# A fused attention and mixture-of-experts kernel: attention in two-bank PSUM tiles, three banks for the second layer, folds in quarters, and batch 1 turned by transfers

## The chip, the cores and the metric

The kernel runs on one core of a Trainium2 chip. The metric is device time in microseconds of one execution (us); lower is better. The profile is one execution recorded by the hardware profiler; its span is a little shorter than the device time of the same execution (543.2 against 544.93 us for the kernel before). In this text PE is TensorE (PEld its weight loads), DVE is VectorE, ACT is ScalarE, POOL is GpSimd and SP is SyncE. In code and profile extracts `...` marks what was left out.

## The reference, cut to what matters

Eight batches of pooled attention, then four experts with two layers each on the 4,608 resulting rows.

```python
# q, k, v: (8 batches, 8 heads, 576, 64)
k_p = k.reshape(B, H, 72, 8, D).mean(axis=3)          # keys and values pooled by 8
v_p = v.reshape(B, H, 72, 8, D).mean(axis=3)
scores = scale * np.matmul(q, k_p.transpose(0, 1, 3, 2))
attn = softmax(scores)                                # exp, divided by its sum
x = (attn @ v_p)  -> transposed to (4608, 512)
# w1: (4, 512, 1024), w2: (4, 1024, 512), p: (4608, 4), normalized
for e in range(4):
    out += p[:, e:e+1] * (np.maximum(x @ w1[e], 0) @ w2[e])
```

## The kernel before

Each batch is a chunk of 512 rows (the 64 rows left of each batch are gathered into a ninth chunk). The experts' matmuls run as a stream. The attention of the next batch is cut into "pieces" that are strewn between the matmuls of the current one, some per slot; there are 32 slots in a chunk (4 experts, 2 halves, 4 gaps).

The PSUM pools have three tiles of one bank each for attention, three for the first layer and two for the second layer:

```python
psum_a = ...tile_pool(name="psum_a", bufs=3, space=PSUM)   # attention
psum_h = ...tile_pool(name="psum_h", bufs=3, space=PSUM)   # first layer
psum_o = ...tile_pool(name="psum_o", bufs=2, space=PSUM)   # second layer
```

Pooling ("folding") keys and values is additions on VectorE. Keys and queries must then be turned; for batches 2 and later a transposing transfer of the DMA engines does it, for batches 0 and 1 TensorE does it and VectorE copies the result out of PSUM:

```python
def by_dma(b):
    return b >= 2

def fold_keys(b, hs):
    raw = raws[("kraw", b)]
    fold(raw, hs)                                  # two additions: 8 -> 4 -> 2
    for dup in range(2):
        nc.vector.tensor_add(out=kps[b % 2][0:SP, hs, dup, :], in0=raw[:, hs, 0, :], in1=raw[:, hs, 1, :])

def keys(b, hs):
    ...
    if by_dma(b):
        nc.sync.dma_start_transpose(out=state[("kpT", b)][:], in_=kps[b % 2][:]...)
        return
    kpt_ps = psum_a.tile([P, H, SP], BF16, tag="a", name="kpt_ps")
    for h in range(hs.start, hs.stop):
        nc.tensor.transpose(kpt_ps[:, h, :], kps[b % 2][0:SP, h], ident[:SP, :SP])
    nc.vector.tensor_copy(out=state[("kpT", b)][:, hs, 0:SP], in_=kpt_ps[:, hs])
# queries(b, pair) and turn(b, r) do the same for q_sb -> qT and for x_tok -> xT

def scores(b, pair):
    both = [psum_a.tile([P, 2, 2, P], F32, tag="a", name="sc_ps") for _ in range(2)]
    ...                                            # four matmuls into the two banks
    exps(b, pair, 0)                               # one exp of 512 for each bank

def divide(c_ps, x_tok, half):                     # one for each half of the heads
    nc.vector.reciprocal(out=inv[:], in_=c_ps[:, :, D])
    nc.vector.tensor_tensor(out=x_tok[:, half], in0=c_ps[:, :, 0:D], in1=inv..., op=ALU.mult)
```

The pieces of a batch:

```python
def opening():
    if by_dma(b): queries(b, 0)
    fold_keys(b, every)                            # all eight heads at once
    if by_dma(b): keys(b, every); load_next()
add(opening)
add(folded_values)                                 # fold_values(b, every), then load_v(b + 1)
if by_dma(b):
    for _ in range(3): add(lambda: None)           # time for the transfers
else:
    add(lambda: keys(b, every)); add(lambda: queried(0))
for pair in range(NPAIR): ...                      # scores, second exp
for r in range(NR): ...                            # contexts, divisions, turning
add(lambda: combine_x(b))                          # the sums of x that the first layer needs
```

The first layer takes seven products in place of eight (`up_seven`). Its result leaves PSUM through ACT copies and through VectorE operations that write `H_sb`; the next products wait for those to free their bank. The weight sums for the products are made on VectorE by `combine_w1(e)`, once per expert, during the first chunk.

The loads are issued on POOL, whose queue is worked in this order:

```python
load_k(0); load_q(0); load_v(0); load_w1(0); load_probs(); load_w1(1); load_w2(0)
load_w1(2); load_w2(1); load_w1(3)
attention_first(); norm_probs(); combine_x(0)
load_k(1); load_q(1); load_v(1); load_w2(2); load_w2(3); load_q_rem(0); load_q_rem(1)
```

The softmax here doesn't subtract the row's maximum and nothing guards it: scores larger than these inputs give would overflow.

## Time and profile before

| | before |
|---|---|
| device time, median of the first 3 runs | 547.04 us (545.41 to 547.12) |
| span of the profiled run | 543.2 us |
| PE busy | 511.9 us, 94% |
| VectorE busy | 322.4 us, 59% |
| PE waits that the waits view lists | kpT's fold 14.4 us, H_sb 4.1 us, others about 8 us |

Three lines of the profile page of the kernel before: busy time by engine, the clock granted to TensorE in 40 equal slices of the span (tenths of full speed), and the chain of work that ended last, as shares of the span.

```profile
PE 511.9 (94%) x3736; PEld 328.7 (61%) x3736; DVE 322.4 (59%) x599; ACT 233.5 (43%) x403; POOL 45.7 (8%) x64
...
PEclk9999899999999999999999999999999999999999
...
PE 84%; DVE 9%; DMA 5%; issue 1%; ACT 0%; POOL 0%; POOLq 0%; DVEq 0%
```

TensorE is the bound. A change can gain only where PE waits, so the next view is the one to read. It is the waits of PE in the kernel before: what waited, for what, then total us, times, longest us.

```profile
PE kpt_ps L182 <- DVE kp L169: 14.4, 3, 7.8
PE g_ps L432 <- DVE H_sb L470: 4.1, 6, 0.8
```

Of the 14.4 us, 10.7 are at the very start; the third one is 3.68 us at 50.6 us, where batch 1's attention starts. The six waits for H_sb come one for each of the batches 2 to 7 (at 106, 155, 219, 268, 331 and 380 us), where the folds of the next batch's keys and values stand between VectorE's H_sb operations.

The same place by stretches of 10 us (busy us and instructions of each engine, then granted clock, DMA share, GB/s), kernel before:

```profile
core 0: us, PE busy (x) PEld busy (x) DVE busy (x) ACT busy (x) POOL busy (x), PEclk, DMA share, GB/s
50.00:60.00 10.00, 5.97 (x32) 3.32 (x30) 6.26 (x10) 0.97 (x2) 0.54 (x1) 0.66 1.30 201
60.00:70.00 10.00, 9.50 (x74) 5.87 (x75) 6.18 (x12) 6.25 (x12) 2.71 (x4) 1.00 1.20 170
70.00:80.00 10.00, 8.76 (x84) 5.90 (x83) 9.08 (x22) 3.22 (x6) 0.00 (x0) 1.00 1.05 126
```

A share of 1.0 and more (with 201, 170 and 126 GB/s) says that the DMA engines are busy throughout until 80 us: the weights of the experts and batch 1's q, k, v are still coming.

### The profile page before, as it was taken

Reading aid. Unit: us, or ns where it says so; the run is one execution under the profiler, and the core shown is the slowest. Engines: PE = TensorE matmul, PEld = TensorE weight load, DVE = VectorE, ACT = ScalarE, POOL = GpSimd, SP = SyncE. Lnnn points to the kernel's source line nnn. Section 1 sums busy time; section 2 is a strip of 40 time slices with the busy share of each in tenths; the row PEclk is TensorE's granted clock in tenths of the full one; section 3 lists DMA queues with packets and bytes.
Section 4 is the critical chain, followed back from the end, with each engine's and each line's share of the span. In section 5 each row is a group of like instructions: output and inputs, shape, how many; then the busy total and the mean of one; then the engine's idle time right before and its main releaser. Section 6 shows DMA issues by size and latency. Waiting matters only on the chain.

```text
span 543.2 us, 9149 instructions
## 1 busy us (share of the span) xinstructions
PE 511.9 (94%) x3736; PEld 328.7 (61%) x3736; DVE 322.4 (59%) x599; ACT 233.5 (43%) x403; POOL 45.7 (8%) x64
## 2 busy tenths in 40 slices
PE   2696999999999999999999999999999999999996
PEld 1354556566656666566666665666566666666663
DVE  3725588837773767367836665568456644554453
ACT  1463343473346333643373345533653345334430
POOL 6632100200110000201100002000000000000000
PEclk9999899999999999999999999999999999999999
DMA  8999980681781014914831119331101010011003
GB/s 122 197 206 200 196 109 1 136 133 31 93 152 38 19 21 111 153 28 70 121 90 23 28 51 165 65 69 32 59 17 25 35 53 1 11 40 39 2 1 77
DMA packets 72954, 40.98 MB, mean 75 GB/s; under 512 B 42688, under 2 KB 68288, under 8 KB 72912
## 3 DMA queue, kind: packets, MB, share of 16 engines
q0 software_dynamic: 33744, 22.63, 29.2%
q1 hardware_dynamic: 39168, 17.77, 14.0%
q8 instruction: 29, 0.48, 0.4%
q14 instruction: 13, 0.11, 0.1%
HBM read 45.16 MB, written 9.44 MB: 101 GB/s over the span
## 4 chain that ended last, share of the span: by engine, by line
PE 84%; DVE 9%; DMA 5%; issue 1%; ACT 0%; POOL 0%; POOLq 0%; DVEq 0%
PE o_ps L501 41%; PE g_ps L432 36%; DMA vraw<-in_v_dram 4%; PE sc_ps L221 2%; DVE H_sb L470 2%; DVE acc L515 2%; PE h_ps L450 2%; PE c_ps L249 1%; DMA kraw<-in_k_dram 1%; DVE vraw L157 1%; DVE kraw L157 1%; DVE vraw L159 1%; PE xt_ps L261 1%; DVE kp L169 1%; DVE x_tok L236 0%
## 5 line engine op out<-in xcount | busy, mean ns | idle before, releaser
L501 PE MATMUL o_ps<-w_bf,H_sb 128*128 128x512 bf16 x1152 | 295.6, 380 | 0.0
L470 DVE CUSTOM_DVE_ANT_0 H_sb<-g_ps,r 128x512 bf16<-128x512 f32 x210 | 143.8, 687 | 162.6 <-ACT r L466 90.3
L432 PEld LDWEIGHTS <-w_bf 128*128 128x128 bf16 x1960 | 185.3, 98 | 75.7 <-issue 11.7
L466 ACT COPY r<-g_ps 128x512 f32<-128x512 f32 x210 | 123.1, 586 | 208.4 <-PE g_ps L432 206.7
L432 PE MATMUL g_ps<-xf,w_bf 128*128 128x256 bf16 x1120 | 157.6, 274 | 6.4 <-DVE H_sb L470 4.1
L501 PEld LDWEIGHTS <-H_sb 128*128 128x128 bf16 x1152 | 113.0, 98 | 76.6 <-issue 0.8
L432 PE MATMUL g_ps<-xT,w_bf 128*128 128x256 bf16 x744 | 101.8, 273 | 0.0
L515 DVE SCALAR_TENSOR_TENSOR acc<-o_ps,p_all,acc 128x512 f32<-128x512 f32 x108 | 80.5, 746 | 21.1 <-PE o_ps L501 21.1
L487 ACT ACTIVATE H_sb<-g_ps 128x512 bf16<-128x512 f32 x70 | 41.8, 598 | 48.2 <-PE g_ps L432 48.2
L228 ACT ACTIVATE expT<-sc_ps 72x512 bf16<-72x512 f32 x64 | 37.1, 592 | 12.5 <-PE sc_ps L221 12.3
L236 DVE TENSOR_TENSOR x_tok<-c_ps,inv 128x256 bf16<-128x256 f32 x72 | 30.6, 425 | 2.5
L92 POOL DMA_DIRECT2D q_sb<-in_q_dram x9 | 7.9, 876 | 237.1 <-DMA qT<-q_sb 230.2
L512 ACT ACTIVATE acc<-o_ps,p_all 128x512 f32<-128x512 f32 x36 | 24.9, 691 | 4.7 <-PE o_ps L501 4.7
L249 PEld LDWEIGHTS <-expT 72*128 72x128 bf16 x256 | 16.2, 102 | 15.3 <-issue 3.1
L235 DVE RECIPROCAL inv<-c_ps 128x4 f32<-128x4 f32 x72 | 12.7, 177 | 14.6 <-PE c_ps L249 11.9
L249 PE MATMUL c_ps<-vp,expT 72*128 72x65 bf16 x256 | 18.4, 200 | 2.8 <-DVE vp L188 2.5
L221 PE MATMUL sc_ps<-qT,kpT 64*72 64x256 bf16 x128 | 14.5, 298 | 1.4 <-DVE qT L210 0.9
L182 PE MATMUL kpt_ps<-ident,kp 72*128 72x72 bf16 x16 | 1.5, 251 | 14.4 <-DVE kp L169 14.4
L221 PEld LDWEIGHTS <-kpT 64*72 64x72 bf16 x128 | 5.4, 111 | 13.8 <-issue 12.9
L157 DVE TENSOR_TENSOR kraw<-kraw 72x2048 bf16<-72x2048 bf16 (+1 forms) x9 | 9.9, 1096 | 5.8 <-DMA kraw<-in_k_dram 5.8
L432 PE MATMUL g_ps<-x_rem,w_bf 128*128 128x256 bf16 x96 | 13.3, 273 | 0.0
L157 DVE TENSOR_TENSOR vraw<-vraw 72x2048 bf16<-72x2048 bf16 (+1 forms) x9 | 9.9, 1095 | 3.7 <-DMA vraw<-in_v_dram 3.7
(54 smaller groups left out, 140.9 us busy)
## 6 DMA issues: line engine op xcount, KB each, us to landing
out_dram<-acc SPq DMA_DIRECT2D x32, 256.0 KB, 2.5
w_bf<-in_moe_w_dram POOLq DMA_DIRECT2D x16, 256.0 KB, 11.3
w_bf<-in_moe_w_dram POOLq DMA_DIRECT2D x4, 1024.0 KB, 18.3
kraw<-in_k_dram POOLq DMA_DIRECT2D x7, 576.0 KB, 10.3
vraw<-in_v_dram POOLq DMA_DIRECT2D x7, 576.0 KB, 11.8
q_sb<-in_q_dram POOLq DMA_DIRECT2D x7, 512.0 KB, 6.9
out_dram<-acc SPq DMA_DIRECT2D x8, 128.0 KB, 2.3
kraw<-in_k_dram POOLq DMA_DIRECT2D x2, 288.0 KB, 5.8
```

What stands on the lines that cost most here:

```text
L157: nc.vector.tensor_add(out=raw[:, hs, 0:4, :], in0=raw[:, hs, 0:4, :], in1=raw[:, hs, 4:8, :])
L221: nc.tensor.matmul(both[r2][0:SP, hh], lhsT=kpT[lo:lo + D, h, 0:SP], rhs=qT[lo:lo + D, h])
L228: nc.scalar.activation(out=state[("expT", b)][:, 2 * pair:2 * pair + 2, :, r2, :], in_=state[("sc", b, pair)][r2][0:SP], func=ACT.Exp, sca ...
L236: nc.vector.tensor_tensor(out=x_tok[:, half], in0=c_ps[:, :, 0:D], in1=inv[:].unsqueeze(2).to_broadcast([P, NPAIR, D]), op=ALU.mult,)
L249: nc.tensor.matmul(c_ps[:, i, :], lhsT=expT[:, h, r // 2, r % 2, :], rhs=vp[:, h, :])
L432: nc.tensor.matmul(bank[:, t, :], lhsT=w1_bf[:, e, block, kc, lo:lo + P], rhs=x[:, kc, :], start=(first and t == 0 and kc == 0), stop=(t = ...
L466: nc.scalar.copy(out=r[:], in_=ps[:])
L470: nc.vector._custom_dve(TENSOR_ADD_SAT, out=out, in0=ps[:], in1=r[:], s0=BIG, s1=0.0)
L487: nc.scalar.activation(out=low[:, :, 0:TH], in_=g[:], func=ACT.Relu)
L501: nc.tensor.matmul(sums[r][:], lhsT=hidden[(c, e)][:, fc, r * P:(r + 1) * P], rhs=w2_bf[:, e, fc, :], start=(fc == 0), stop=(fc == FCH - 1),)
L512: nc.scalar.activation(out=accs[(c, r)][:], in_=o_ps[:], func=ACT.Copy, scale=prob)
L515: nc.vector.scalar_tensor_tensor(out=dst, in0=o_ps[:], scalar=prob, in1=dst, op0=ALU.mult, op1=ALU.add,)
```

## The change

The intent: use one instruction over two banks where there were two (one exp of 1024, one reciprocal and one multiply per row block); free one bank for a third tile of the second layer; spread the burst of folds over four pieces; and take batch 1's turning off TensorE and VectorE by letting the DMA engines do it. The core of the diff:

```diff
-psum_a bufs=3, psum_o bufs=2
+psum_a bufs=1, psum_o bufs=3              # one attention tile, of two banks
+    def two_banks():
+        return psum_a.tile([P, 2, NT], F32, tag="a", name="two")

     def by_dma(b):
-        return b >= 2
+        return b >= 1

     scores:
-        both = [psum_a.tile([P, 2, 2, P], F32, tag="a", name="sc_ps") for _ in range(2)]
+        two = two_banks()
         ... four matmuls ...
+        nc.scalar.activation(out=dst, in_=two[0:SP]..., func=ACT.Exp, scale=EXP_SCALE)

-    def divide(c_ps, x_tok, half):          # twice per row block
+    def divide(banks, x_tok):               # once per row block, both banks
+        nc.vector.reciprocal(out=inv[:], in_=c_ps[:, :, :, D])
+        nc.vector.tensor_tensor(out=x_tok[:], in0=c_ps[:, :, :, 0:D], in1=inv..., op=ALU.mult)

     attention(b):
-        add(opening)                        # query transfer, fold of all keys, key transfer
-        add(folded_values)
+        add(lambda: (turn_queries(), fold_keys(b, lo)))
+        add(keyed)                          # fold_keys(b, hi), key transfer, load_next
+        add(lambda: fold_values(b, lo))
+        add(folded_values)                  # fold_values(b, hi), load_v(b + 1)
     # [cut: half of the first batch's score and context tiles come from the other two pools;
     #  the remainder chunks likewise use the two-bank tile]
```

What stays TensorE's to turn (the first batch's keys and x) takes its tiles from the attention pool as before, so those now come from the single two-bank tile.

More of the change, by code (lines that the diff above doesn't have):

```diff
@@ L60 @@
     rpool = ctx.enter_context(tc.tile_pool(name="rpool", bufs=6))
-    psum_a = ctx.enter_context(tc.tile_pool(name="psum_a", bufs=3, space=bass.MemoryType.PSUM))
+    psum_a = ctx.enter_context(tc.tile_pool(name="psum_a", bufs=1, space=bass.MemoryType.PSUM))
     psum_h = ctx.enter_context(tc.tile_pool(name="psum_h", bufs=3, space=bass.MemoryType.PSUM))
-    psum_o = ctx.enter_context(tc.tile_pool(name="psum_o", bufs=2, space=bass.MemoryType.PSUM))
+    psum_o = ctx.enter_context(tc.tile_pool(name="psum_o", bufs=3, space=bass.MemoryType.PSUM))
     w1_bf = wpool.tile([P, E, 7, 2, FH], BF16, name="w1_bf")
@@ L154, with one_bank @@
     state = {}
+    def two_banks():
+        return psum_a.tile([P, 2, NT], F32, tag="a", name="two")
+    def one_bank(n):
+        pool, tag = ((psum_h, "h_ps"), (psum_o, "o_ps"))[n % 2]
+        return pool.tile([P, NT], F32, tag=tag, name="one")
     def fold(raw, hs):
@@ L215, in scores @@
             state[("expT", b)] = apool.tile([SP, H, 2, 2, P], BF16, name="expT", bufs=1)
-        both = [psum_a.tile([P, 2, 2, P], F32, tag="a", name="sc_ps") for _ in range(2)]
+        expT = state[("expT", b)]
+        apart = b == 0 and pair % 2
+        if apart:
+            both = [one_bank(n)[:] for n in range(2)]
+        else:
+            two = two_banks()
+            both = [two[:, n] for n in range(2)]
         for hh in range(2):
@@ L221, in scores, with divide_half @@
                 nc.tensor.matmul(
-                    both[r2][0:SP, hh], lhsT=kpT[lo:lo + D, h, 0:SP], rhs=qT[lo:lo + D, h]
-                )
-        state[("sc", b, pair)] = both
-        exps(b, pair, 0)
-    def exps(b, pair, r2):
+                    both[r2][0:SP].rearrange("j (h r p) -> j h r p", h=2, r=2)[:, hh],
+                    lhsT=kpT[lo:lo + D, h, 0:SP], rhs=qT[lo:lo + D, h],
+                )
+        dst = expT[:, 2 * pair:2 * pair + 2].rearrange("j h r s p -> j s (h r) p")
+        if apart:
+            for n in range(2):
+                nc.scalar.activation(
+                    out=dst[:, n], in_=both[n][0:SP].rearrange("j (a p) -> j a p", p=P),
+                    func=ACT.Exp, scale=EXP_SCALE,
+                )
+            return
         nc.scalar.activation(
-            out=state[("expT", b)][:, 2 * pair:2 * pair + 2, :, r2, :],
-            in_=state[("sc", b, pair)][r2][0:SP], func=ACT.Exp, scale=EXP_SCALE,
-        )
-    def divide(c_ps, x_tok, half):
-        inv = npool.tile([P, NPAIR], F32, name="inv")
+            out=dst, in_=two[0:SP].rearrange("j s (a p) -> j s a p", p=P),
+            func=ACT.Exp, scale=EXP_SCALE,
+        )
+    def divide(banks, x_tok):
+        c_ps = banks[:, :, 0:NPAIR * (D + 1)].rearrange("p a (h d) -> p a h d", h=NPAIR)
+        inv = npool.tile([P, 2, NPAIR], F32, name="inv")
+        nc.vector.reciprocal(out=inv[:], in_=c_ps[:, :, :, D])
+        nc.vector.tensor_tensor(
+            out=x_tok[:], in0=c_ps[:, :, :, 0:D],
+            in1=inv[:].unsqueeze(3).to_broadcast([P, 2, NPAIR, D]), op=ALU.mult,
+        )
+    def divide_half(bank, x_tok, half):
+        c_ps = bank[:, 0:NPAIR * (D + 1)].rearrange("p (h d) -> p h d", h=NPAIR)
+        inv = npool.tile([P, NPAIR], F32, name="invh")
         nc.vector.reciprocal(out=inv[:], in_=c_ps[:, :, D])
@@ L239, in divide, with context_half @@
         )
-    def context(b, r, half):
+    def context_half(b, r, half, bank):
         expT, vp = state[("expT", b)], vps[b % 3]
-        if ("x", b, r) not in state:
-            state[("x", b, r)] = npool.tile([P, 2, NPAIR, D], BF16, name="x_tok", bufs=5)
-        pool, tag = (psum_h, "h_ps") if b == 0 and half else (psum_a, "a")
-        c_ps = pool.tile([P, NPAIR, D + 1], F32, tag=tag, name="c_ps")
         for i in range(NPAIR):
@@ L249, in context, with context_first @@
             nc.tensor.matmul(
-                c_ps[:, i, :], lhsT=expT[:, h, r // 2, r % 2, :], rhs=vp[:, h, :]
-            )
-        divide(c_ps, state[("x", b, r)], half)
+                bank[:, i * (D + 1):(i + 1) * (D + 1)],
+                lhsT=expT[:, h, r // 2, r % 2, :], rhs=vp[:, h, :],
+            )
+    def context(b, r):
+        x_tok = npool.tile([P, 2, NPAIR, D], BF16, name="x_tok", bufs=5)
+        state[("x", b, r)] = x_tok
+        banks = two_banks()
+        for half in range(2):
+            context_half(b, r, half, banks[:, half])
+        divide(banks, x_tok)
+    def context_first(r, half):
+        if half == 0:
+            state[("x", 0, r)] = npool.tile([P, 2, NPAIR, D], BF16, name="x_tok", bufs=5)
+        bank = one_bank(r)
+        context_half(0, r, half, bank[:])
+        divide_half(bank[:], state[("x", 0, r)], half)
     def flip(x_tok, dst, on_dma, copy=nc.vector.tensor_copy):
@@ L271, in rem_queries @@
         q_rem = q_rems.pop(i)
-        qTr = apool.tile([P, NPAIR, 2, REM], BF16, name="qTr")
+        qTr = apool.tile([P, NPAIR, 2, REM], BF16, name="qTr", bufs=1)
         nc.sync.dma_start_transpose(
@@ L280, in rem_scores @@
         qTr = state.pop(("qTr", i))
-        both = [psum_a.tile([P, 2, NPAIR, REM], F32, tag="a", name="scr_ps") for _ in range(2)]
+        two = two_banks()
         for bb in range(2):
@@ L285, in rem_scores @@
                 for hh in range(2):
-                    lo = hh * D
+                    lo, at = hh * D, (bb * NPAIR + pair) * REM
                     nc.tensor.matmul(
-                        both[hh][0:SP, bb, pair, :], lhsT=kpT[lo:lo + D, 2 * pair + hh, 0:SP],
+                        two[0:SP, hh, at:at + REM], lhsT=kpT[lo:lo + D, 2 * pair + hh, 0:SP],
                         rhs=qTr[lo:lo + D, pair, bb, :],
                     )
-        expTr = apool.tile([SP, 2, 2, NPAIR, REM], BF16, name="expTr")
-        for hh in range(2):
-            nc.scalar.activation(out=expTr[:, hh], in_=both[hh][0:SP],
-                                 func=ACT.Exp, scale=EXP_SCALE)
+        expTr = apool.tile([SP, 2, 2, NPAIR, REM], BF16, name="expTr", bufs=1)
+        nc.scalar.activation(
+            out=expTr[:].rearrange("j a b h t -> j (a b h t)"),
+            in_=two[0:SP].rearrange("j a n -> j (a n)"), func=ACT.Exp, scale=EXP_SCALE,
+        )
         state[("expTr", i)] = expTr
@@ L299, in rem_context @@
         x_tok = npool.tile([P, 2, NPAIR, D], BF16, name="x_tok", bufs=5)
+        banks = two_banks()
         for half in range(2):
-            c_ps = psum_a.tile([P, NPAIR, D + 1], F32, tag="a", name="c_ps")
             for j in range(NPAIR):
@@ L305, in rem_context @@
                     nc.tensor.matmul(
-                        c_ps[bb * REM:(bb + 1) * REM, j, :],
+                        banks[bb * REM:(bb + 1) * REM, half, j * (D + 1):(j + 1) * (D + 1)],
                         lhsT=expTr[:, h % 2, bb, h // 2, :], rhs=vps[(2 * i + bb) % 3][:, h, :],
                     )
-            divide(c_ps, x_tok, half)
+        divide(banks, x_tok)
         state[("xr", i)] = x_tok
@@ L325, in attention_first @@
                 scores(0, pair - 1)
-                exps(0, pair - 1, 1)
         scores(0, NPAIR - 1)
-        exps(0, NPAIR - 1, 1)
         for half, hs in enumerate((lo, hi)):
@@ L331, in attention_first @@
             for r in range(NR):
-                context(0, r, half)
+                context_first(r, half)
                 if half and r:
@@ L337, in attention @@
     def attention(b):
-        every = slice(0, H)
+        lo, hi = (slice(i * H // 2, (i + 1) * H // 2) for i in range(2))
         more = b + 1 < B
@@ L342, in attention, with rest, turn_queries @@
         add = pieces.append
-        def opening():
+        def rest():
+            add(lambda: None)
+        def turn_queries():
             if by_dma(b):
                 queries(b, 0)
-            fold_keys(b, every)
-            if by_dma(b):
-                keys(b, every)
-                load_next()
         def load_next():
@@ L356, in load_next, with keyed @@
                 load_k(b + 1)
+        def keyed():
+            fold_keys(b, hi)
+            if by_dma(b):
+                keys(b, slice(0, H))
+                load_next()
         def folded_values():
-            fold_values(b, every)
+            fold_values(b, hi)
             if more:
@@ L366, in queried @@
                 load_next()
-        add(opening)
+        add(lambda: (turn_queries(), fold_keys(b, lo)))
+        add(keyed)
+        add(lambda: fold_values(b, lo))
         add(folded_values)
         if by_dma(b):
-            for _ in range(3):
-                add(lambda: None)
+            rest()
+            rest()
         else:
-            add(lambda: keys(b, every))
+            add(lambda: keys(b, slice(0, H)))
             add(lambda: queried(0))
@@ L379, in attention @@
             add(lambda pair=pair: scores(b, pair))
-            add(lambda pair=pair: exps(b, pair, 1))
+            if by_dma(b):
+                rest()
         for r in range(NR):
-            add(lambda r=r: context(b, r, 0))
-            add(lambda r=r: context(b, r, 1))
+            add(lambda r=r: context(b, r))
             if by_dma(b):
@@ L391, in attention @@
             for _ in range(3):
-                add(lambda: None)
+                rest()
         add(lambda: combine_x(b))
```

## The prediction

> **What bounds the kernel now.** TensorE. The page's busy table has PE at 511.9 of 543.2 us; by 10 us stretches it is at 10.00 in most from 110 us on; the chain of waits is 84% PE. VectorE (59%) and ScalarE (43%) have room on average. Only three places can give time:
>
> 1. The first batch, 0–37 us: PE waits for loads and VectorE.
> 2. The start of batch 1's attention, 50–90 us. In the waits view PE waits 3.7 us for batch 1's folded keys (load landed at 51.5 us); VectorE then sits in its queue for the values (landed at 56.73). PE idles 4 us in 50–60 with its clock at 0.66, and 2 us more in 70–90, where VectorE is 91–96% busy.
> 3. Six waits of PE for VectorE's H_sb, 4.1 us in all, one per later batch: folding keys and values (2.7 + 2.3 us) passes VectorE in one burst.
>
> **What the change does.**
> - Division: before, two reciprocals (177 ns) and two multiplies (425 ns), 1.20 us per row block; after, one each, by my estimate from these 0.18 + 0.69 = 0.87 us. Saves 1.3 us of VectorE per batch, mostly off the chain.
> - Exp: two of 512 took 1.08 us back to back; [...] Hardly a gain.
> - Third bank for the second layer: no PE wait for o_ps shows, so no gain.
> - One two-bank buffer for three banks: scores wait for the previous exp, contexts for the previous division. Later batches place them two slots (3.3 us) apart, which hides it. Batch 1 places them one slot (1.6 us) apart, its first division behind 2.8 us of weight sums: 1–1.5 us of new PE waits.
> - Folds in four pieces instead of two: the burst spreads over four slots; most of place 3 goes: -3.5 us.
> - Batch 1 by transfers: removes 40 PE transposes (about 2.4 us) and 3.8 us of VectorE copies. But its scores now wait for the query load (about 54 us), then for transposing transfers that took 4.5–4.9 us to land later, with emptier queues; here DMA share is 1.2–1.3, so I estimate 6–8 us, landing at 60–63. PE gets there at about 55.5, so the idle stretch moves and grows to 5–7 us, and the clock drops again; but PE is one slot further on. Net for 50–90 us: -2 to +3 us, about +0.5 with the new waits.
> - First batch: turning x has one buffer instead of three, +0.7 us, hidden behind loads landing at 51–57 us.
>
> **Sum.** -3.5 (bursts) +0.5 (batch 1) -0.5 (rest) = -3.5 us. Predicted 543.5 us, 538 to 549 eight times in ten. Faster by over 2%: 0.07; within: 0.89; slower: 0.04.
>
> **What would show it.** The H_sb waits of PE (4.1 us) fall under 1.5 us. PE idles 4–8 us around 55–63 us for the transfers of qT or kpT, PEclk low behind it. Reciprocals of 8 near 0.18 us, multiplies of 512 near 0.69[...]. The period of two later batches (112.55 us between key folds in the chain) falls by 1–1.4 us. In 70–90 us VectorE is under 85% busy.
>
> **What would make it wrong.** Transposing transfers landing by 58 us: up to 4 us better. Starved behind weight loads until 66 us: slower than before. The single two-bank buffer stalling PE in every batch, where the division queues behind other VectorE work: several us slower. The long exp delaying ScalarE's copies until PE waits: up to 2 us slower.

The sum stands: -3.5 +0.5 -0.5 = -3.5 us, from 547.0 (the first median of before) to 543.5. For the 0.69 us of the merged multiply the trace before has a VectorE operation of the same 128x512: H_sb, 687 ns on average.

## More of the kernel before

One burst of folds on VectorE in the kernel before (start, duration, operation), to be compared later:

```profile
101.31 0.68 DVE L470 CUSTOM_DVE_ANT_0 H_sb<-g_ps,r 128x512 bf16<-128x512 f32 x1
101.91 0.74 DVE L515 SCALAR_TENSOR_TENSOR acc<-o_ps,p_all,acc 128x512 f32<-128x512 f32 x1
102.57 1.21 DVE L157 TENSOR_TENSOR vraw<-vraw 72x2048 bf16<-72x2048 bf16 x1
...
104.88 0.74 DVE L515 SCALAR_TENSOR_TENSOR acc<-o_ps,p_all,acc 128x512 f32<-128x512 f32 x1
105.54 1.27 DVE L470 CUSTOM_DVE_ANT_0 H_sb<-g_ps,r 128x512 bf16<-128x512 f32 x2
```

Between the H_sb operation at 101.31 and the next one at 105.54, VectorE does 3.6 us of other work (101.91 to 105.54). At 106.27 us PE has waited 0.81 us for that second H_sb.

## The result, and the profile after

| | before | after |
|---|---|---|
| device time, median of 4 runs | 546.22 us | 558.75 us (558.50 to 558.83) |
| ratio | | 1.0228 [1.0206, 1.0251] |
| span of the profiled run | 543.2 us | 556.9 us |
| PE busy | 511.9 us | 509.4 us |
| VectorE busy | 322.4 us | 318.3 us |

The change is slower by 12.5 us, although it removed work from TensorE, VectorE and ScalarE. It lies outside the predicted range (538 to 549).

The same three page lines, kernel after:

```profile
PE 509.4 (91%) x3696; PEld 325.9 (59%) x3696; DVE 318.3 (57%) x575; ACT 230.4 (41%) x369; POOL 45.7 (8%) x64
...
PEclk9999679999999999999999999999999999999999
...
PE 76%; DMA 12%; DVE 9%; issue 1%; POOL 1%; ACT 1%; POOLq 0%; DVEq 0%
```

The chain has 12% of DMA where it had 5%, and the clock row has a dip to 6 and 7 in slices 5 and 6. The waits of PE in the kernel after name the place:

```profile
PE two L234 <- DMA kpT<-kp: 16.4, 1, 16.4
PE kpt_ps L189 <- DVE kp L176: 10.7, 2, 7.8
PE g_ps L477 <- DVE H_sb L515: 6.0, 9, 0.8
...
PE xt_ps L300 <- ACT xT L301: 1.6, 3, 0.7
```

One wait of 16.4 us for batch 1's transposed keys takes the place of the 3.7 us wait for its folded keys. The waits for H_sb rose from 4.1 to 6.0 us. By stretches, kernel after (columns as before):

```profile
50.00:60.00 10.00, 5.43 (x35) 3.05 (x32) 8.89 (x19) 2.02 (x4) 0.00 (x0) 0.94 1.27 202
60.00:70.00 10.00, 0.00 (x0) 0.00 (x0) 1.84 (x4) 0.00 (x0) 0.00 (x0) 0.50 1.42 161
70.00:80.00 10.00, 7.59 (x46) 4.17 (x47) 1.38 (x2) 4.52 (x6) 3.19 (x4) 0.71 1.01 123
```

PE does nothing from 60 to 70 us, and comes back at a lowered clock. The granted clock was 0.50 in the idle stretch; it reached this at 58.8 us, 2.8 us after PE's last matmul ended (56.0 us). In before the same took 2.0 us (50.6 to 52.6). Full clock came back at 75.9 us, 3.5 us after PE's restart at 72.41.

How much of the loss is here? A marker that both traces have is the first weight sum of the last opening step on VectorE: it starts at 88.46 us before and at 99.80 us after (VectorE's timelines, before first):

```profile
88.46 0.68 DVE L409 TENSOR_TENSOR w_bf<-w_bf 128x1024 bf16<-128x1024 bf16 x1
```

```profile
99.80 0.68 DVE L454 TENSOR_TENSOR w_bf<-w_bf 128x1024 bf16<-128x1024 bf16 x1
```

So 11.3 of the 13.7 us of the profiled spans are lost before the marker. (2.1 of them were lost already in the first batch: the same matmul group starts at 49.15 us before and at 51.29 after. But the wait behind swallows them, as e2 below shows: with the first batch of before it waits 18.5 us in place of 16.4, and loses as much.) The rest of the program (the span less the marker's time) takes 454.7 us before and 457.1 us after: 2.4 us, of which the H_sb waits explain 1.9.

Where did the 16.4 us come from? First SP's timeline of the kernel after, the two issues (start, us that the issue occupied the queue), then, from its view of DMA issues in 50 to 75 us, the sizes and the us from issue to landing:

```profile
53.89 1.43 SPq L204 DMA_TRANSPOSE qT<-q_sb  x1
56.35 9.07 SPq L183 DMA_TRANSPOSE kpT<-kp  x1
```

```profile
qT<-q_sb SPq DMA_TRANSPOSE x1, 17.3
kpT<-kp SPq DMA_TRANSPOSE x1, 16.0
```

The transfers were issued when their inputs were ready, but landed 17.3 and 16.0 us later. The keys landed at 72.35 us (56.35 + 16.0) and PE's scores start at 72.41. In a later batch, where the queue of loads (q0) is empty, the same two transfers land in 4.4 and 2.7 us (DMA issues, kernel after, 226 to 233 us):

```profile
qT<-q_sb SPq DMA_TRANSPOSE x1, 4.4
kpT<-kp SPq DMA_TRANSPOSE x1, 2.7
```

What they share the engines with is in the DMA view of 58 to 62 us, kernel after (packets, MB, share of the 16 engines' time; q0 carries the loads issued on POOL, q1 everything issued on SP):

```profile
DMA packets 1240, 0.78 MB, mean 196 GB/s; under 512 B 630, under 2 KB 1240, under 8 KB 1240
...
q0 software_dynamic: 623, 0.62, 91.7%
q1 hardware_dynamic: 617, 0.16, 29.6%
```

The two queues get 623 and 617 packets: one for one. But a packet of the loads has about 1 KB here (0.62 MB in 623) and one of the transposing transfers about 256 bytes (0.16 MB in 617), so the loads get four fifths of the bytes. From these counts one can work out the order of the time: the two transfers put 2,752 packets on q1 between 50 and 75 us; at 617 packets per 4 us that is an estimate of 17.8 us. From the first issue to the last landing it took 18.5 us, but that the two are so near is in part luck. Hardly a packet (15) came before 58 us, 4 us after the first issue, and why is not shown; the rest needed only some 14 us, because the rate rose later, to 677 packets in the 3 us from 66 to 69. The counts stayed about one for one there (664 packets of loads, now small ones too, 0.21 MB). In e3 below, from 59 to 61 us, when no other packets moved, such transfers moved 2,107 packets in 2 us: 1,054 per us, against 154 here.

Last, the costs of the merged instructions, from the page's groups of the kernel after (busy us, mean ns):

```profile
L246 ACT ACTIVATE expT<-two 72x1024 bf16<-72x1024 f32 x30 | 30.6, 1019 | 27.6 <-PE two L234 27.5
...
L255 DVE TENSOR_TENSOR x_tok<-two,inv 128x512 bf16<-128x512 f32 x32 | 22.1, 692 | 1.1
...
L254 DVE RECIPROCAL inv<-two 128x8 f32<-128x8 f32 x32 | 6.5, 204 | 13.7 <-PE two L273 10.5
```

The multiply and the reciprocal are as predicted: 0.69 us (0.69) and 0.20 us (0.18). The exp takes 1.02 us, where two of 512 took 1.08 us back to back in before.

### The profile page after: what moved, and what is told of

It is laid out like the page before. It is cut to its first block, busy times and chain, and to the rows that moved or that the text cites. A ratio compares the mean times of both kernels' runs of the same rounds, so it can differ in the third digit from the quotient of the medians.

```text
span 556.9 us, 9030 instructions
## 1 busy us (share of the span) xinstructions
PE 509.4 (91%) x3696; PEld 325.9 (59%) x3696; DVE 318.3 (57%) x575; ACT 230.4 (41%) x369; POOL 45.7 (8%) x64
## 4 chain that ended last, share of the span: by engine, by line
PE 76%; DMA 12%; DVE 9%; issue 1%; POOL 1%; ACT 1%; POOLq 0%; DVEq 0%
PE o_ps L546 38%; PE g_ps L477 35%; DMA w_bf<-in_moe_w_dram 4%; DMA vraw<-in_v_dram 3%; DMA kpT<-kp 3%; DVE H_sb L515 2%; DVE acc L560 2%; PE two L234 2%; PE two L273 1%; DMA kraw<-in_k_dram 1%; DVE kraw L164 1%; DVE kp L176 1%; ACT r L511 1%; DVE kraw L166 1%; DVE vraw L164 1%
## 5 line engine op out<-in xcount | busy, mean ns | idle before, releaser
L246 ACT ACTIVATE expT<-two 72x1024 bf16<-72x1024 f32 x30 | 30.6, 1019 | 27.6 <-PE two L234 27.5
L234 PE MATMUL two<-qT,kpT 64*72 64x256 bf16 x120 | 13.0, 296 | 16.5 <-DMA kpT<-kp 16.4
L255 DVE TENSOR_TENSOR x_tok<-two,inv 128x512 bf16<-128x512 f32 x32 | 22.1, 692 | 1.1
L273 PEld LDWEIGHTS <-expT 72*128 72x128 bf16 x256 | 13.0, 102 | 11.8 <-issue 3.7
L254 DVE RECIPROCAL inv<-two 128x8 f32<-128x8 f32 x32 | 6.5, 204 | 13.7 <-PE two L273 10.5
L164 DVE TENSOR_TENSOR kraw<-kraw 72x1024 bf16<-72x1024 bf16 x16 | 10.9, 679 | 4.8 <-DMA kraw<-in_k_dram 4.8
L273 PE MATMUL two<-vp,expT 72*128 72x65 bf16 x224 | 11.9, 194 | 1.0 <-DVE x_tok L255 1.0
L117 POOL DMA_DIRECT2D w_bf<-in_moe_w_dram x16 | 11.3, 717 | 9.4 <-DMA w_bf<-in_moe_w_dram 8.1
L164 DVE TENSOR_TENSOR vraw<-vraw 72x1024 bf16<-72x1024 bf16 x16 | 10.9, 678 | 1.8 <-DMA vraw<-in_v_dram 1.8
## 6 DMA issues: line engine op xcount, KB each, us to landing
w_bf<-in_moe_w_dram POOLq DMA_DIRECT2D x16, 256.0 KB, 11.9
```

The lines of the kernel that those rows point to most:

```text
L164: nc.vector.tensor_add(out=raw[:, hs, 0:4, :], in0=raw[:, hs, 0:4, :], in1=raw[:, hs, 4:8, :])
L234: nc.tensor.matmul(both[r2][0:SP].rearrange("j (h r p) -> j h r p", h=2, r=2)[:, hh], lhsT=kpT[lo:lo + D, h, 0:SP], rhs=qT[lo:lo + D, h],)
L246: nc.scalar.activation(out=dst, in_=two[0:SP].rearrange("j s (a p) -> j s a p", p=P), func=ACT.Exp, scale=EXP_SCALE,)
L255: nc.vector.tensor_tensor(out=x_tok[:], in0=c_ps[:, :, :, 0:D], in1=inv[:].unsqueeze(3).to_broadcast([P, 2, NPAIR, D]), op=ALU.mult,)
L273: nc.tensor.matmul(bank[:, i * (D + 1):(i + 1) * (D + 1)], lhsT=expT[:, h, r // 2, r % 2, :], rhs=vp[:, h, :],)
```

## The experiments

The main theory (A; T in the first texts): the loss is batch 1's transposing transfers, slowed by the queued weight loads. A rival (B; P there): it is the single two-bank buffer that stalls PE. For the later H_sb waits: that what counts is how much other VectorE work stands between two H_sb operations (G), against the size of one fold. On chips 1, 2, 11 and 12 kernel before ran, with medians 544.83, 544.39, 544.76 and 545.13 us. All twelve kernels gave correct results. Differences are clear of noise where an interval leaves out 1, as all but e8's do.

| run | what it is | us | ratio to before |
|---|---|---|---|
| e1 | after, batch 1 back on PE | 554.02 | 1.0161 [1.0125, 1.0198] |
| e2 | before, batch 1 by transfers | 557.21 | 1.0226 [1.0182, 1.0270] |
| e3 | after, two weight loads held back | 554.11 | 1.0155 [1.0118, 1.0192] |
| e4 | before, batch 1 loaded earlier | 542.21 | 0.9940 [0.9908, 0.9972] |
| e5 | e1, and PE's turning in tiles of the second layer's pool | 547.49 | 1.0049 [1.0029, 1.0068] |
| e6 | e5 with whole folds | 560.18 | 1.0282 [1.0249, 1.0314] |
| e7 | e4, batch 1's keys turned later | 540.88 | 0.9929 [0.9903, 0.9956] |
| e8 | e5, at most one quarter-fold per slot | 544.78 | 0.9985 [0.9948, 1.0021] |
| e9 | e7 with quarter-folds, one per slot | 552.02 | 1.0128 [1.0092, 1.0165] |
| e10 | e8 with e7's loads and order | 539.40 | 0.9898 [0.9868, 0.9928] |
| e11 | e10 with one-bank tiles | 539.23 | 0.9888 [0.9866, 0.9910] |
| e12 | e10 again, twin of e11 | 539.26 | 0.9891 [0.9868, 0.9915] |

### e1: after, batch 1 turned by TensorE again

```diff
     def by_dma(b):
-        return b >= 1
+        return b >= 2
```

> The changed kernel with batch 1 turned on TensorE again (transfers only from batch 2 on); all else as changed. Theory T (the loss is batch 1's transposing transfers, landing late): the 16.4 us wait of PE for kpT goes, and the time falls to 544-549 us, within 0.7% of before. Rival P (the loss is the single two-bank PSUM buffer and its waits): the time stays at 554 us or more. Either way PE's waits for H_sb tell whether the steady stages are better than before's 4.1 us.

Measured 554.02 us. The big wait is gone, but only 0.7% of the 2.3% comes back: theory A's 544 to 549 us was missed. The waits of PE in e1 show a new one that neither kernel had:

```profile
PE qt_ps L213 <- DVE kpT L190: 5.2, 1, 5.2
...
PE qt_ps L213 <- ACT expT L246: 2.2, 2, 1.1
```

Turning the queries on PE takes a PSUM tile in this program, and the attention pool has only one, which the turned keys (5.2 us) and then the scores' exps (2.2 us) hold. So rival B is also right, but for a path that the change itself does not take: the change closed the old path for batch 1 and took a worse one.

### e2: before, with only batch 1 by transfers

```diff
     def by_dma(b):
-        return b >= 2
+        return b >= 1
```

> The kernel before with only batch 1 turned by transfers (before's PSUM pools, exps, divisions and fold pieces). Theory T: nearly the whole loss appears, 556-561 us, with PE idle 10 us or more for qT or kpT, which land 14-18 us after issue. Rival P: 545-549 us.

Measured 557.21 us: this one line alone costs 2.3%, as much as the whole change (the two intervals overlap almost fully). Waits of PE, and the landing of the two transfers (DMA issues, 50 to 75 us), both of e2:

```profile
PE sc_ps L221 <- DMA kpT<-kp: 18.5, 1, 18.5
```

```profile
qT<-q_sb SPq DMA_TRANSPOSE x1, 15.6
kpT<-kp SPq DMA_TRANSPOSE x1, 15.2
```

This kernel has neither the two-bank buffer nor the quarter-folds. Theory A holds without them. That it is the queued loads that slow the transfers is for e3 to show.

### e3: after, the last two weight loads held back

```diff
-        load_w2(2)                 # from the opening
-        load_w2(3)
     def load_next():               # in batch 1, after load_q(2)
+                if b == 1:
+                    load_w2(2)
+                    load_w2(3)
```

> The changed kernel, but the loads of the last two second-layer weights (2 MB in SBUF) are issued behind batch 2's query load, which waits for qT of batch 1, so that they are not in the queue when batch 1's transposing transfers run. If theory T is right and those loads are what starves the transfers: qT and kpT land within 5-9 us of issue instead of 17.3 and 16.0, PE's wait falls from 16.4 to 3-7 us, and the time to 546-551 us (it may lose a few us to a new wait for those weights). If the transposing transfers are slow by themselves: still 12 us or more to landing, and 556 us or more.

Measured 554.11 us. On POOL load_q(2) waits until batch 1's qT is there (it is issued at 61.66 us) and the two weight loads follow it (62.80), so the weights now come behind the two transfers. The landing times in e3 (DMA issues, 50 to 75 us) fall to what the prediction had guessed, and PE's wait is 5.8 us:

```profile
qT<-q_sb SPq DMA_TRANSPOSE x1, 5.1
kpT<-kp SPq DMA_TRANSPOSE x1, 4.3
```

This shows directly that the queued loads are what slows the transfers. Yet the ratio is only 0.7% better than the change's, and the expected 546 to 551 us was missed, because the same thing then happens to the next transposing transfers: batch 1's x. VectorE waits for them, and PE behind it for H_sb (lines of e3's VectorE and PE timelines):

```profile
91.56 0.43 DVE L468 TENSOR_TENSOR xf<-xT 128x512 bf16<-128x512 bf16 x1 [7.55 <-DMA xT<-x_tok]
```

```profile
93.78 1.86 PE L480 MATMUL g_ps<-xT,w_bf 128*128 128x256 bf16 x8 [6.04 <-DVE H_sb L518]
```

Holding the loads back moved the collision to a later transfer; it did not remove it. PE also waited 1.2 us for a weight that now came late.

### e4: before, with batch 1's loads ahead of the last first-layer weights

```diff
         load_w2(1)
-        load_w1(3)
         attention_first()
         ...
         load_v(1)
+        load_w1(3)
```

> The kernel before with one change of order: batch 1's key, query and value loads are issued ahead of the first-layer weights of expert 3 (1 MB in SBUF), which are needed only at about 72 us. Tests that before's own idle 4 us at 50-60 us (and half clock behind it) is the late landing of batch 1's keys and values. Expected: keys land by 45 us, the 3.7 us wait of PE for the folded keys falls under 1 us, and the time falls by 5-9 us, to 537-541 us. If the wait was set by VectorE's queue instead: within 2 us of before.

Measured 542.21 us, 0.6% faster than before, less than the 537 to 541 us expected. If batch 1 is held up by its loads, the answer is to change their order, not to add more transfers. PE's wait for batch 1's folded keys fell only from 3.68 to 2.50 us: the fold now starts at 51.24 us, behind the weight sums on VectorE, where it started at 51.51 for want of its load. But the values no longer hold VectorE up: their fold starts at 53.89 instead of 56.75 us, and PE is busy 7.44 of the 10 us from 50 to 60, where it was 5.97.

### e5: e1, with PE's turning in tiles of the second layer's pool

```diff
-        kpt_ps = psum_a.tile([P, H, SP], BF16, tag="a", name="kpt_ps")
+        kpt_ps = psum_o.tile([P, H, SP], BF16, tag="o_ps", name="kpt_ps")
-        pool, tag = (psum_o, "o_ps") if b == 0 else (psum_a, "a")      # qt_ps
+        pool, tag = psum_o, "o_ps"
-        xt_ps = psum_a.tile([P, NPAIR, P], BF16, tag="a", name="xt_ps")
+        xt_ps = psum_o.tile([P, NPAIR, P], BF16, tag="o_ps", name="xt_ps")
```

> The run with batch 1 on TensorE again still took 554.0 us: its trace shows PE waiting inside batch 1 for kpT, exp and xT copies (5.2 + 2.2 + 1.1 + 1.1 + 1.0 us), because the turning tiles and the scores and contexts all share the one two-bank buffer. Here it is repeated with the turning tiles of keys, queries and x in the second layer's three banks. If sharing the one buffer was the rest of the loss: those waits fall under 3 us in all and the time to 545-549 us. If the rest lies elsewhere (exp, division or folds): still 552 us or more. PE's H_sb waits should stay near 6 us.

Measured 547.49 us. The path over TensorE with tiles of its own is 1.1% better than e1 and 1.8% better than the change. What is left over before is 0.5%, and e5's H_sb waits are those of the change, 6.0 us in 9 waits. The tiles are not free either: PE waits 3.7 us for one that a sum of the second layer (acc) still holds, and 1.1 us for an exp, so the waits in batch 1 did not quite fall under the 3 us expected.

### e6: e5 with whole folds

```diff
-        add(lambda: (turn_queries(), fold_keys(b, lo)))
-        add(keyed)
-        add(lambda: fold_values(b, lo))
+        add(lambda: (turn_queries(), keyed()))     # keyed and folded_values now fold all heads
         add(folded_values)
         if by_dma(b):
-            rest(); rest()
+            for _ in range(4): rest()
```

> The run before this one, with the folds of keys and values whole again (two pieces, with two rests in place of the two removed for the transferred batches). My prediction said that four pieces take away PE's H_sb waits; the changed kernel has 6.0 us of them, before 4.1. If the pieces are to blame (they cost VectorE about 0.95 us more per batch, 3.2 + 2.8 against 2.7 + 2.3 us): H_sb waits fall to 3-4.5 us and the time by 1-3 us. If the two-bank exp and division are: they stay near 6 us.

Measured 560.18 us, 2.3% slower than e5, where 1 to 3 us less were expected. So in this pacing quarters are better than wholes. In before, with another pacing and other tiles, whole folds cost PE only 4.1 us of H_sb waits. VectorE's timeline of e6 shows why:

```profile
104.68 0.69 DVE L513 CUSTOM_DVE_ANT_0 H_sb<-g_ps,r 128x512 bf16<-128x512 f32 x1 [1.80 <-ACT r L509]
105.29 0.74 DVE L558 SCALAR_TENSOR_TENSOR acc<-o_ps,p_all,acc 128x512 f32<-128x512 f32 x1
105.95 1.21 DVE L164 TENSOR_TENSOR kraw<-kraw 72x2048 bf16<-72x2048 bf16 x1
...
109.25 1.21 DVE L164 TENSOR_TENSOR vraw<-vraw 72x2048 bf16<-72x2048 bf16 x1
...
111.56 0.68 DVE L513 CUSTOM_DVE_ANT_0 H_sb<-g_ps,r 128x512 bf16<-128x512 f32 x1
```

The key fold and the value fold both fall between two H_sb operations: 6.3 us of other work (105.29 to 111.56) against 3.6 in before. (The 5.6 us of e8's text is the same gap without the first operation, on acc.) PE's timeline of e6 shows the price:

```profile
112.30 1.87 PE L475 MATMUL g_ps<-xf,w_bf 128*128 128x256 bf16 x8 [2.63 <-DVE H_sb L513]
```

An equal group of eight matmuls took 1.04 us at 102.99 and 1.87 us here. After 2.63 us of idling the granted clock is lowered (0.83 on average from 110 to 120 us): the second layer's matmuls average 459 ns from 113 to 119 us and 379 ns from 130 to 136. So this wait cost more than itself; behind waits of 0.81 us in before (100 to 110 us) and 0.83 us in after (115 to 125 us) the mean granted clock stayed at 1.00. The H_sb waits of e6 sum to 10.0 us, 4.0 more than e5's, and the kernel is 12.7 us slower (11.9 us in the profiled spans). The records divide the 11.9 us: all of PE's listed waits sum to 36.9 us in e6 and 28.7 in e5, 8.2 more (H_sb 4.0, kpT's fold 1.8, weight sums 1.3, others 1.1), and PE is busy 512.4 against 508.7 us with nearly the same number of matmuls on record (3,670 and 3,671), 3.7 more. That the lowered clock is the cause of all these 3.7 us was not shown.

### e7: e4, with batch 1's keys turned some pieces later

```diff
         add(opening)
-        add(folded_values)
         if by_dma(b):
+            add(folded_values)
             ...
         else:
+            for _ in range(3):
+                add(lambda: None)
             add(lambda: keys(b, every))
+            add(folded_values)
             add(lambda: queried(0))
```

> The early-loads run (542.2 us) met less than half of what I expected: keys landed at 48 us, but VectorE folded them only at 51.2-54.0 us, behind the weight sums, and PE still waited 2.5 us for them. Here the same kernel, with three empty pieces between the fold of batch 1's keys and their turning on TensorE, and the fold of the values after that turning. If PE's wait is only one of order: the wait at 50-56 us falls under 1 us, the granted clock stays at 1.0, and the time falls by 2-5 us, to 537-540 us. If the late pieces crowd VectorE instead: 541-544 us.

Measured 540.88 us, ratio 0.9929; the interval overlaps e4's, so a gain over e4 is likely but not shown. PE's wait for batch 1's folded keys shrank from 2.50 us in e4 to 0.55, as expected, because PE does other work until VectorE is through. But a wait of 1.8 us for qT is new against e4, the mean clock from 50 to 60 us is 0.90 and not 1.0, and the time lies just outside the expected 537 to 540 us.

### e8: e5, with at most one quarter-fold per slot and none in the third

```diff
     def slot(n):
         due += per_slot
+        folded = False
         while pieces and due >= 1.0:
+            if getattr(pieces[0], "fold", False):   # the four fold pieces are marked
+                if folded or n == 2:
+                    break
+                folded = True
             pieces.popleft()()
             due -= 1.0
```

> The 547.5 us run (changed kernel, batch 1 on TensorE with its own turning tiles), with one rule for the folds of the later batches: at most one quarter-fold per slot, and none in the third slot of four, so that VectorE's queue has an H_sb operation after every quarter. VectorE's work is the same. Theory G (PE waits when too much lies between two H_sb in VectorE's order: 4.5 us gave 0.84 us of wait, 5.6 us gave 2.6, 3.6 gave 0.8): H_sb waits of PE fall from 6.0 to under 1.5 us and the time to 543-546 us. Rival (VectorE has too much work near the folds, whatever the order): waits stay at 4-6 us and the time within 1 us.

Measured 544.78 us; e5's loss is gone (0.9985 against 1.0049). By the order of `up_seven`, no VectorE H_sb stands between the third and the fourth gap, because that part of H_sb is made on ACT; so two pieces, one in each of these gaps, fall between the same two H_sb operations. The rule forbids that. The H_sb waits fell from 6.0 us (9 waits) to 3.4 us (6), where the theory had said less than 1.5 us. So theory G gives the direction, and not the size. VectorE's timeline of e8 suggests why, though no run tests it: from 103.27 to 112.3 us VectorE works without a gap, and there an H_sb operation and a quarter-fold take 2.0 to 2.2 us together, where a slot of PE is 1.6 us by the prediction's figure (in before, four slots without attention pieces take 6.51 us, 482.82 to 489.33). VectorE falls behind over the four quarters, and PE waits 0.66 us at 110.40. So the rival, too much work near the folds in any order, is in part right.

### e9: e7 with quarter-folds and the same rule

```diff
-        add(opening); add(folded_values); three empty pieces      # batches 2 and later
+        add(alone(lambda: (queries(b, 0), fold_keys(b, lo))))
+        add(alone(keyed))                  # fold_keys(b, hi), keys(b, every), load_next()
+        add(alone(lambda: fold_values(b, lo)))
+        add(alone(last_values)); two empty pieces
```

> The kernel before with early loads and later turning of keys (540.9 us), plus quarter-folds under the rule of the run before this one; one-bank attention tiles, two exps and two divisions as before. Theory G: H_sb waits fall from 4.1 to under 1 us, the time to 535-538.5 us. Rival: 540-542 us.

Measured 552.02 us: a miss, and an instructive one. The H_sb waits do fall to 0.7 us, as theory G says (in part because in batch 2 the H_sb operation at 104.13 us falls into PE's wait for kpT, from 103.10 to 106.43, which hides it). But holding back the second half of the key fold holds back the transfer of the keys behind it, and PE then waits for that (waits of PE, e9):

```profile
PE sc_ps L221 <- DMA kpT<-kp: 9.7, 3, 4.0
...
PE g_ps L454 <- DVE H_sb L492: 0.7, 3, 0.2
```

The transfer there is issued after batch 2's query transfer by 5.0 us, where it was 1.9 us in before. A wait of 3.4 us in all was traded for one of 9.7. The clock dips behind these waits too (0.85 from 100 to 110 us).

### e10: e8, with e7's loads and its order in batch 1

```diff
-        load_w1(3)                          # moved behind load_v(1), as in e4
         if by_dma(b): ...                   # the four marked quarter-folds, as in e8
         else:
+            add(lambda: fold_keys(b, slice(0, H)))
+            for _ in range(3): rest()
             add(lambda: keys(b, slice(0, H)))
+            add(lambda: (fold_values(b, lo), folded_values()))
             add(lambda: queried(0))
```

> The changed kernel's two-bank tiles, single exp and single division and three second-layer banks, with batch 1 on TensorE, turning tiles in the second layer's banks, early loads, later turning of keys and the fold rule: the twin of the run before this one but for the two-bank tiles. It tells what the two-bank tiles themselves are worth. If they are worth nothing or cost a little through the single buffer in batches 0 and 1: 0-4 us slower than its twin. If the 1.3 us of VectorE that they save per batch counts: 1-3 us faster.

Measured 539.40 us, 1.0% faster than before: two-bank tiles, third bank, quarter-folds with the rule, batch 1 on TensorE and its loads early. Its 50 to 60 us has PE busy for 8.85 us at full clock (5.97 us at 0.66 in before). Its twin e9 was spoiled by the wait for kpT, so this pair doesn't tell what the tiles are worth. The next pair does.

### e11 and e12: the tiles alone

e11 is e10 with one-bank tiles (three for attention, two for the second layer), exps of 512 and one division per half; the list of pieces, the pacing, the loads and the fold rule are untouched. e12 is e10 again.

```diff
-psum_a bufs=1, psum_o bufs=3;  two = two_banks();  one exp of 1024, one division
+psum_a bufs=3, psum_o bufs=2
+        both = [psum_a.tile([P, NT], F32, tag="a", name="sc_ps")[:] for _ in range(2)]
+        for n in range(2): nc.scalar.activation(out=dst[:, n], in_=both[n][0:SP]..., func=ACT.Exp)
+        for half in range(2): divide_half(bank[:], x_tok, half)      # own bank for each half
```

> The tenth kernel with its attention in one-bank tiles again: three banks for attention and two for the second layer, two exps of 512 back to back and two divisions per row block in place of one of each; list of pieces, pacing, loads and fold rule untouched. Theory T (in this schedule the tiles are worth nothing, their extra VectorE work of about 10 us in all is off the chain): within 1.5 us of its twin. Rival U (the merged division does help, because it shortens what stands in VectorE's queue): 2 to 4 us slower than its twin, with more PE waits for H_sb than 3.6 us. Rival V (three attention banks help where batch 1 and the first batch turn through tiles): 1.5 to 4 us faster, with the first batch's second layer start about 1.5 us earlier.

> The tenth kernel again, unchanged, as the twin of the run above on the same chip and in the same rounds: 0.987 to 0.993 of before, as the first time (0.9898).

Measured 539.23 and 539.26 us: the same, and e12 repeats e10. VectorE is busy 326.6 us in e11 and 320.7 us in e12, so the merged division does save about 6 us of VectorE, and the H_sb waits are the same 3.6 us in 7 waits. The part that gave the change its name, the two-bank tiles with the merged operations and the third bank, is worth nothing in time in this schedule; it saves work that nobody waits for.

## Why the prediction was wrong, point by point

**The step that failed** is the one on batch 1: "here DMA share is 1.2–1.3, so I estimate 6–8 us, landing at 60–63 ... the idle stretch moves and grows to 5–7 us ... Net for 50–90 us: -2 to +3 us". The mechanism was right, and the size of one term was off. The transfers took 17.3 and 16.0 us to land, the idle stretch was 16.4 us, and the stretch up to the marker lost 11.3 us. e2 shows that this one line costs the whole loss by itself, and e3 shows that without the queued weights the transfers land in 5.1 and 4.3 us. The estimate scaled the landing by how full the engines looked. It should have counted packets: as the trace after shows, these small packets went one for one with the large ones (617 and 623 in 4 us) and so got a small part of the bytes (0.16 of 0.78 MB). The trace before has the rate: it moves 7,659 packets from 50 to 75 us, 306 per us, and with half of these for the transfers, 2,752 packets (the count in after) take 18 us, an estimate that is nearer than 6 to 8. The prediction did list "Starved behind weight loads until 66 us: slower than before" among what could make it wrong. This is what happened, until 72 us.

**The folds.** "The H_sb waits of PE (4.1 us) fall under 1.5 us", worth 3.5 us: wrong. They rose to 6.0 us, and after the marker the program lost 2.4 us instead of gaining 3.5. The period of two later batches rose from 112.55 to 113.30 us (PE's waits at 106.27 and 218.82 before, 117.58 and 230.88 after), where a fall by 1 to 1.4 us was predicted. More pieces of half the size do not help if they still come two at a time between H_sb operations. VectorE's timeline of the kernel after:

```profile
112.38 0.74 DVE L560 SCALAR_TENSOR_TENSOR acc<-o_ps,p_all,acc 128x512 f32<-128x512 f32 x1
113.03 0.68 DVE L164 TENSOR_TENSOR kraw<-kraw 72x1024 bf16<-72x1024 bf16 x1
...
115.27 0.68 DVE L164 TENSOR_TENSOR kraw<-kraw 72x1024 bf16<-72x1024 bf16 x1
...
116.85 0.68 DVE L515 CUSTOM_DVE_ANT_0 H_sb<-g_ps,r 128x512 bf16<-128x512 f32 x1
```

Both key quarters fall into one gap of 4.5 us (112.38 to 116.85; 3.6 in before), and the value quarters delay H_sb once more: PE waits 0.83 us at 117.58 and 0.54 us at 121.53, where before it waited once. This second wait comes in the batches 2, 4 and 6 alone; it makes the nine waits of the six. e6 (10.0 us), e8 (3.4) and e9 (0.7) support the gap as a cause, but its length is not the whole of it: the gaps of 3.6 us before and 4.5 us here gave the same wait (0.81 and 0.83 us).

**The single two-bank buffer.** The predicted 1 to 1.5 us of new waits in batch 1 did not decide anything: 1.0 us for x_tok shows, elsewhere hidden. But the prediction did not see that the single buffer shuts the path over TensorE, which cost 1.1% in e1 against e5.

**Right:** the durations of the merged reciprocal (0.20 us) and multiply (0.69 us), and that the merged exp (1.02 us) hardly gains (e11 against e12, for all the merged operations together: nothing). Right too: no gain from the third bank; no wait for an o_ps bank shows in either kernel.

**The first batch.** The predicted +0.7 us for turning x in one buffer shows as 1.6 us of waits for xT in 3 waits. The first layer starts at 26.77 us instead of 25.22. In which part that is due to the loads of that run isn't settled: the same point lies at 24.00 in e12 and at 25.99 in e11, which have the same time.

**Open.** For the 3.4 us of H_sb waits that e8 keeps there is only the reading of its timeline. Why the transfers' first packets came 4 us after the issue is not known. Nor is it shown how much of e9's loss is the lowered clock and how much the waits; the number of matmuls on record differs between it and e7 (3,736 and 3,670), so that their busy times can't be compared.

## What to carry to other kernels

Before handing a transposition to the DMA engines, look at what else is queued at that moment and count packets, not bytes or engine share: the transfers that took 3 to 5 us in a quiet stretch took 16 to 17 us next to weight loads, whose packets moved one for one with theirs (623 and 617 in 4 us, 0.62 and 0.16 MB), and the granted clock of the idle TensorE then fell to 0.50 as well. Work on VectorE that is not on the chain still has to be placed: what counted here is how much of it stood between two operations that free TensorE's banks (with 6.3, 4.5 and 3.6 us of it PE waited 2.63, 0.83 and 0.81 us), so pace it by those and not by its piece size, and look at what the delayed piece starts (here a transfer). A change with several parts can hide a good one behind a bad one, and an idle resource (here the saved 6 us of VectorE) is worth nothing until something waits for it; the gain here (e4, e7, e10) lay in the order of the loads and of batch 1's pieces, which was not part of the change.
